# FFN weight scales from ScalarE's sums of squares, x's transposes issued one tile later, the product copies in a buffer of their own, and the queues laid out anew

## The chip, the cores and the metric

The kernel runs on one core of a Trainium2 chip. A core has TensorE (in the profile PE for its matmuls, PEld for its weight loads), VectorE (DVE), ScalarE (ACT), GpSimd (POOL) and SyncE (SP, whose work is to issue DMAs). Each engine takes its instructions in the order in which the program lists them. The metric is the device time of one execution, in microseconds. Lower is better.

## The reference

The input x has 2048 rows of 576. It is normalised, goes through windowed attention with 32 heads of 18, and the result is gated by a bilinear feed-forward network (FFN) of width 4608.

```python
# _A_ref: qkv = x @ wqkv; softmax over the last 256 positions, causal; ... @ wo
# _B_ref:
    g = jnp.einsum("bsd,df->bsf", x, w_gate)
    u = jnp.einsum("bsd,df->bsf", x, w_up)
    h = g * u
    return jnp.einsum("bsf,fd->bsd", h, w_down)
# the whole:
    x = A_x
    xn = _layernorm(x, axis=-1)
    s = _A_ref(xn, A_wqkv, A_wo)
    g = _silu(_B_ref(xn, B_w_gate, B_w_up, B_w_down))
    return x + s * g
```

All inputs and outputs are float32.

## The kernel before

**Arithmetic.** Every float32 matrix is split into two float16 matrices, a high part and a low part, and a product is made of three float16 matmuls (high by high, high by low, low by high). So that the parts fit float16, each weight matrix is first multiplied by a power of two. `power` works it out from a bound on the matrix's largest magnitude: it clears the mantissa bits and takes the reciprocal. The high part is made by ScalarE (`hi`, L139), the low part by VectorE (`lo`, L142), which subtracts the high part from the scaled source.

**Prologue.** The rows of x come in 16 tiles of 128. For a tile, `stats`, `root` and `newton` give mean and deviation, `norm2` writes the normalised tile and its split `xh` (ScalarE, and GpSimd for the low part, L222 and L223), and `turn` (L226) transposes `xh` into `XT` by a DMA that SyncE issues. V is made tile by tile (`v_pass`, L307). Then q and k are made for the first 1024 rows (half 0) and later for the other 1024 (half 1): `qk_tile` runs 14 matmuls for one of 9 blocks of 128 columns (m) and one of two blocks of 512 rows, ScalarE and VectorE write the result into the tile `qp` (two buffers), and `qk_store` (L353) sends the finished tile m to DRAM in eight DMAs. Between two of these blocks `aside` does other work. In half 0 it is the preparation of x's tiles 8 to 15 through `pair`, whose step number n grows by one from block to block: `stats` at 0 and 1, `norm2` and `turn` of the first tile at 2, of the second at 3. In half 1 it is, among others, the first FFN group's scale (`ffn_amax`, `ffn_spread_out`, `ffn_spread_in`, `ffn_scale`). `keep_warm` runs matmuls on zeros whose result nobody reads. At the very start TensorE takes `v_full(0)` and `v_full(1)` (L500), then `spread_pe` (L447), which brings the bound of V's weights to one partition.

**Memory.** The prologue's tiles lie in the pools `qpool` and `pro`, which are closed behind the last q/k block. The pool `late` and the attention pool are opened in the same memory, so a tile of theirs waits until the tiles that lay there have had their last use. `late` holds the FFN's accumulator `acc`, the split down weights `dnw`, the hidden values `hh` and the ring `ft` of four tiles of 128x512, into which the FFN's products are copied. `const` and `ring` are open throughout.

**Main loop.** There are 72 slots: 18 groups of 256 FFN columns (g), and in each group four slots (two blocks of 128 columns, k, by two halves of 1024 rows, q). A slot computes seven products P1 to P7 into the two PSUM banks A and C (`prod`, `mm`, L844). The products come out of the banks by ScalarE's `copy_out` (L872) and VectorE's `add_out` (L876) and `times_0` (L880); GpSimd's `times_1` (L884) makes the second half of the hidden values; `h_hi` (L888) and `h_lo` (L892) split them. Eight `down` units (L908) of three slots before run in between, each drained by `down_out` (L918, L920) on VectorE; most share one bank `dn`. Slots 1 to 64 also carry one attention step each: scores (L715), maxima (`score`, L724), exponentials (`probs`, L729 and L731), their split (`probs_hi` L736, `turn_probs` L745 with a transposing DMA L748), the product with V (`weigh`, L757) and `finish` (L769 to L778).

The weights of group g are loaded three slots ahead of its first slot (`ffn_raw`), that is in a slot whose number is 1 modulo 4. Their bounds are taken there and in the slot behind it (`ffn_amax`, L372: six reductions to the largest magnitude, three matrices by two halves; `ffn_spread_out`, L377, combines the halves and stores them; `ffn_spread_in` reads them back on all partitions; `ffn_scale`, L385 and `power`, makes the scales). GpSimd then forms scaled sums of the weights (`ffn_ratio` L393, `ffn_sums` L404). The splits of the weights (`w_hi`, `w_lo`, `dn_hi`, `dn_lo`, `dn_low`) stand in the slots 3 and 0 modulo 4, and one of them in 1.

**Order.** The order on every engine is set by hand: `at(slot, t, f, ...)` gives each call a due time of slot x 18.65 + t, and the list is sorted by it. The times of most calls that are not matmuls stand in the table `W`. They set the order alone; an instruction runs when its engine reaches it and its inputs are there.

```python
    for n in range(6):
        at(b - 3, W["amax"][n], ffn_amax, g, (1, 1, 2, 2, 0, 0)[n], n % 2)
    at(b - 3, W["so"], ffn_spread_out, g)
    at(b - 3, W["si"], ffn_spread_in, g)
    at(b - 2, W["scale"], ffn_scale, g)
```

Of the kernel before, what the change touches and what calls it, by code (L numbers as in the profile page):

```python
# [8 lines left out]
F32 = mybir.dt.float32  # L9
FR = mybir.dt.float32r  # L10
BF = mybir.dt.bfloat16
F16 = mybir.dt.float16
AF = mybir.ActivationFunctionType
OP = mybir.AluOpType
AX = mybir.AxisListType
# [5 lines left out]
def kernel(  # L21
# [10 lines left out]
    nc = tc.nc  # L32
    x = x[0]
    out = out[0]
    S, D = x.shape
# [9 lines left out]
    scale = DH ** -0.5  # L45
# [11 lines left out]
    WF = 2.0 ** 12  # L57
# [5 lines left out]
    LEAST, MOST = 2.0 ** -60, 2.0 ** 60  # L63
# [22 lines left out]
    ps_o = const.tile([128, 4], F32, name="ps_o")  # L86
    sig = const.tile([128, 4], F32, name="sig")

    def wq_ring():
        return pro.tile([128, 10, 128], F16, name="wq", bufs=9)  # L90

# [11 lines left out]
    def keep_warm(n):  # L103
        ps = bank("pv", 1)
        for _ in range(n):
            nc.tensor.matmul(ps, idle[:, 0:128], idle, start=True, stop=True)
# [5 lines left out]
    def power(m, p, s, top):  # L112

        nc.vector.tensor_scalar(p, m, LEAST, MOST, op0=OP.max, op1=OP.min)
        pi = p.bitcast(mybir.dt.int32)
        nc.vector.tensor_scalar(pi, pi, 0x7F800000, None, op0=OP.bitwise_and)
        nc.vector.reciprocal(s, p)
        nc.vector.tensor_scalar(s, s, top, None, op0=OP.mult)

# [105 lines left out]
    def turn(t):  # L225
        nc.sync.dma_start(XT[:, :, t * 128:(t + 1) * 128], XH.pop(t), transpose=True)  # L226
# [97 lines left out]
    UW, DW, RAW, SC, SW = {}, {}, {}, {}, {}  # L324
# [42 lines left out]
    def ffn_amax(g, kind, half):  # L367
        if (g, "am") not in SC:
            SC[g, "am"] = ring.tile([128, 2, 3], F32, name="am", bufs=2)
        r = RAW[g, kind]  # L370
        r = r[:, half] if kind == 2 else r[:, :, half * 128:(half + 1) * 128]
        nc.vector.tensor_reduce(SC[g, "am"][:, half, kind:kind + 1], r, axis=AX.X if kind == 2 else AX.XY,  # L372
                                op=OP.max, apply_absolute_value=True)

    def ffn_spread_out(g):
        am = SC.pop((g, "am"))
        nc.vector.tensor_tensor(am[:, 0], am[:, 0], am[:, 1], op=OP.max)  # L377
        spread_out(f"f{g}", am[:, 0], 3)

    def ffn_spread_in(g):  # L380
# [2 lines left out]
    def ffn_scale(g):  # L383
        sc = SC[g] = ring.tile([128, 12], F32, name="sc", bufs=3)
        nc.vector.tensor_reduce(sc[:, 0:3], SC.pop((g, "sp")), axis=AX.X, op=OP.max)  # L385
        power(sc[:, 0:3], sc[:, 3:6], sc[:, 6:9], WF)
        nc.gpsimd.tensor_tensor(sc[:, 10:11], sc[:, 3:4], sc[:, 7:8], op=OP.mult)
        nc.gpsimd.tensor_tensor(sc[:, 9:10], sc[:, 3:4], sc[:, 4:5], op=OP.mult)
        nc.gpsimd.tensor_scalar(sc[:, 9:10], sc[:, 9:10], sc[:, 5:6], C_FFN, op0=OP.mult, op1=OP.mult)
# [55 lines left out]
    def spread_pe(col, k):  # L445
        tp = bank("dn", 1)
        nc.tensor.transpose(tp[0:1, 0:128], col, ident)  # L447
        nc.vector.tensor_reduce(mrow[:, k:k + 1], tp[0:1, 0:128], axis=AX.X, op=OP.max)
# [46 lines left out]
    def v_full(k):  # L495
        if k == 0:
            PV[0] = [bank(*VB[j]) for j in range(2)]
        r = slice(0, 128 if k < 4 else 64)
        for j in range(2):
            nc.tensor.matmul(PV[0][j][:, :HALF], x32[r, k], rv[r, k, j * HALF:(j + 1) * HALF],  # L500
                             start=k == 0, stop=k == 4)

    for k in range(2):
        v_full(k)
    spread_pe(ps_v[:, 0:1], 0)
    norm2(2)
    turn(2)
# [56 lines left out]
    def pair(p, n):  # L564

        if n == 1:
            stats(2 * p + 1)
            root(2 * p, 2)
            newton(2 * p, 2)
        elif n == 0:  # L570
            stats(2 * p)
        elif n in (2, 3):
            norm2(2 * p + n - 2)
            turn(2 * p + n - 2)

    def aside(half, n):

# [22 lines left out]
    for t in range(16):  # L600
        if t % 8 > 3 or t >= 8:
            v_pass(t, 0, 4)
            if t == 7:
                tp = spread_pe2(1, "up", 2)
            v_pass(t, 4, 14)
            if t == 6:
                spread_pe(am_qk[:, 5:6], 1)
            if t == 6:
                v_store(0)
            if t == 7:  # L610
                qk_scale(tp)
                x_load(8)
                x_load(9)
        if t % 8 > 0 and t > 2:
            v_out(t - 1)
        if t in (2, 4):
            amax(am_qk[:, t // 2:t // 2 + 1], rqk[:, t // 2])
        elif t in (3, 5):
            k = (t + 5) // 2 - 1
            square(am_qk[:, k:k + 1], rqk[:, k])  # L620
        if t == 5:
            nc.scalar.activation(am_qk[:, 3:5], am_qk[:, 3:5], AF.Sqrt)
            nc.vector.tensor_reduce(am_qk[:, 5:6], am_qk[:, 0:5], axis=AX.X, op=OP.max)
        if t >= 8:
            for p in range(4):
                t_form(p, t - 8 - 2 * p)
        if t % 8 < 7:
            continue
        half = t // 8
        if half == 0:  # L630
            qk_split(0)
            qk_split(1)
        v_out(t)
        for m in range(QM):
            for c in (2 * half, 2 * half + 1):
                qk_tile(UW["q", m], m, c)
                aside(half, 2 * m + c % 2)
            qk_store(m, half)
            if half == 0:
                if m < 7:  # L640
                    v_store(m + 1)
                if m in (0, 2, 4):
                    x_load(10 + m)
                    x_load(11 + m)
                if m == 8:
                    for kind in range(3):
                        for part in range(2):
                            ffn_raw(0, kind, part)
            else:
                if m == 2:  # L650
                    ffn_spread_out(0)
                if m == 3:
                    ffn_spread_in(0)
                del UW["q", m]
# [8 lines left out]

    def h_ring():
        return late.tile([128, 2, 512], F16, name="hh", bufs=8)

    def f_ring():
        return late.tile([128, 512], F32, name="ft", bufs=4)

    att = att_stack.enter_context(tc.tile_pool(name="att", bufs=1))  # L670
    bias = att.tile([128, 384], BF, name="bias")
# [119 lines left out]

    NSLOT = NG * NCH
    T = 18.65
    W = {"ttr": [-1.02, -0.99, 2.9, 3.58, 7.44, 8.28, 9.7, 10.61], "exp": [0.73, 4.02, 9.94, 10.85], "cast": [1.61, 4.85, 10.71, 12.76], "plo": [3.33, 6.32, 12.48, 13.35], "fin": 8.64, "whi": [6.17, 10.44, 7.03, 16.67], "wlo": [9.12, 13.19, 15.36, 18.08], "dhi": 16.48, "dlo": 18.02, "dlow": 18.26, "sum0": [15.56, 19.68, 19.83], "sum1": [-8.02, 0.5, 6.85], "amax": [11.14, 11.93, 14.37, 14.25, 18.11, 18.75], "scale": 14.47, "hhi0": 18.41, "hlo0": 22.9, "hhi1": 21.52, "hlo1": 23.66, "h1": 18.28, "pv": [16.98, 7.67], "x": 7.18, "raw0": 11.17, "so": 21.83, "si": 24.97}
    todo = []

    def at(slot, t, f, *a):
# [325 lines left out]
```

## Time and profile before

| | us |
|---|---|
| median of 3 runs | 1631.88 |
| lowest, highest | 1630.68, 1631.97 |
| the profiled execution, whole | 1631.18 |
| its span in the profile | 1629.5 |

The profile is that of one execution. The page gives busy time by engine; the timeline gives instructions in order of time, merged where they are alike, with the idle time of the engine ahead of them and what ended it in brackets (`[2.76 <-DVE qp L344]`); the groups give for each line and shape the count, the busy time, the mean duration in ns, and behind a bar the idle time before; the view of one line gives the least, median and greatest duration in ns. `L844` is line 844 of the kernel. The ends of matmuls are modelled and overlap a little.

### The profile page before, as it was taken

To read this page: it belongs to the slowest core of one execution; us is meant where nothing else is said; L and a number is where in the kernel's file an instruction comes from. 1 tells how busy PE (TensorE), PEld (TensorE's weight loads), DVE (VectorE), ACT (ScalarE), POOL (GpSimd) and SP (SyncE) were. 2 spreads that over 40 slices of the span, in tenths; PEclk is the share of its full clock that TensorE was granted. 3 is DMA by queue.
4 is the path that set the end of the run, shared out by engine and by line. 5 is a ranking of instruction groups with operands and counts; after the bars stand their busy time and mean duration, and the time that the engine had idled before them with its cause. 6 is when DMAs were issued, how large, how long until landed. Compare 5 with 4: busy or idle time off the path is not lost.

```text
span 1629.5 us, 32463 instructions
## 1 busy us (share of the span) xinstructions
PE 1585.4 (97%) x11875; PEld 905.3 (56%) x11875; DVE 1360.3 (83%) x2989; ACT 923.2 (57%) x1742; POOL 815.0 (50%) x823
## 2 busy tenths in 40 slices
PE   9999989999999999999999999999999999999999
PEld 5455335555555555555555555555555555555577
DVE  7546478898989899998989898999998999977564
ACT  6433366565666666576666566666666666623230
POOL 3122346555565757565656566665656574723000
PEclk9999999999999999999999999999999999999999
DMA  8473365555647576857666666666675757540435
GB/s 235 116 181 126 88 125 109 110 118 110 130 82 152 114 159 107 169 105 150 127 131 138 124 133 133 135 132 141 126 145 109 160 108 157 106 115 2 103 79 170
DMA packets 551457, 206.06 MB, mean 126 GB/s; under 512 B 492544, under 2 KB 532096, under 8 KB 551296
## 3 DMA queue, kind: packets, MB, share of 16 engines
q1 hardware_dynamic: 551296, 203.98, 59.0%
q8 instruction: 93, 1.52, 0.4%
q14 instruction: 68, 0.56, 0.1%
HBM read 76.63 MB, written 23.75 MB: 62 GB/s over the span
## 4 chain that ended last, share of the span: by engine, by line
PE 47%; DVE 29%; issue 4%; DMA 3%; ACT 2%; SPq 1%; POOL 0%; ACTq 0%; DVEq 0%; POOLq 0%
PE up L844 25%; PE dn L908 9%; PE s L908 6%; DVE acc L920 5%; DVE ws L142 4%; DVE ft L876 3%; PE pv L757 3%; DVE hh L892 3%; DVE wu L142 2%; PE s L1013 2%; DVE dnw L142 2%; PE s L715 2%; DMA raw<-in_B_w_gate_dram 2%; PE up L1013 1%; DVE am L372 1%
## 5 line engine op out<-in xcount | busy, mean ns | idle before, releaser
L908 PEld LDWEIGHTS <-hh 128*128 128x128 f16 x3456 | 329.1, 98 | 180.6 <-issue 25.5
L908 PE MATMUL dn<-dnw,hh 128*128 128x288 f16 x2070 | 310.3, 286 | 14.7 <-DVE acc L920 14.0
L844 PEld LDWEIGHTS <-ws 128*128 128x128 f16 x1872 | 178.2, 98 | 187.5 <-issue 32.1
L844 PE MATMUL up<-XT,ws 128*128 128x512 f16 x1008 | 273.2, 381 | 1.2 <-DVE ft L876 1.2
L844 PE MATMUL up<-XT,wg 128*128 128x512 f16 x1008 | 254.6, 382 | 1.5 <-DVE ft L880 1.2
L844 PE MATMUL up<-TX,ws 128*128 128x512 f16 x864 | 211.6, 381 | 6.1 <-ACT ft L872 6.1
L888 ACT ACTIVATE hh<-ft 128x512 f16<-128x512 f32 x144 | 90.6, 629 | 221.6 <-DVE ft L880 219.8
L920 DVE SCALAR_TENSOR_TENSOR acc<-dn,sc,acc 128x288 f32<-128x288 f32 x325 | 166.1, 511 | 53.6 <-PE dn L908 53.0
L908 PE MATMUL s<-dnw,hh 128*128 128x288 f16 x1386 | 203.9, 286 | 0.0
L876 DVE SCALAR_TENSOR_TENSOR ft<-up,ft 128x512 f32<-128x512 f32 x216 | 147.4, 683 | 32.4 <-PE up L844 26.9
L872 ACT ACTIVATE ft<-up 128x512 f32<-128x512 f32 x216 | 126.4, 585 | 83.5 <-PE up L844 75.7
L729 ACT ACTIVATE mx<-mx 128x2 f32<-128x2 f32 x256 | 52.0, 203 | 195.7 <-DVE mx L724 194.5
L884 POOL TENSOR_TENSOR ft<-ft 128x512 f32<-128x512 f32 x72 | 92.5, 1285 | 135.1 <-DVE ft L876 102.8
L892 DVE SCALAR_TENSOR_TENSOR hh<-hh,ft 128x512 f16<-128x512 f16 x144 | 149.9, 1041 | 0.2 <-ACT hh L888 0.2
L844 PEld LDWEIGHTS <-wg 128*128 128x128 f16 x1008 | 99.2, 98 | 84.8 <-issue 5.7
L920 DVE SCALAR_TENSOR_TENSOR acc<-s,sc,acc 128x288 f32<-128x288 f32 x219 | 111.6, 510 | 27.2 <-PE s L908 27.1
L844 PEld LDWEIGHTS <-wu 128*128 128x128 f16 x720 | 70.1, 97 | 94.1 <-issue 30.5
L339 PE MATMUL up<-XT,wq 128*128 128x512 f16 x504 | 111.4, 383 | 6.0 <-DVE qp L344 5.9
L757 PEld LDWEIGHTS <-pt 128*128 128x128 f16 x2880 | 86.2, 96 | 47.6 <-issue 30.2
L844 PE MATMUL up<-TX,wu 128*128 128x512 f16 x432 | 105.0, 379 | 0.0
L844 PE MATMUL up<-XT,wu 128*128 128x512 f16 (+1 forms) x288 | 98.0, 381 | 0.0
L757 PE MATMUL pv<-vt,pt 128*128 128x37 f16 x2880 | 93.4, 179 | 0.8 <-DMA vt<-v_d 0.8
(1225 smaller groups left out, 2774.6 us busy)
## 6 DMA issues: line engine op xcount, KB each, us to landing
raw<-in_B_w_down_dram SPq DMA_DIRECT2D x36, 288.0 KB
raw<-in_B_w_gate_dram SPq DMA_DIRECT2D x36, 256.0 KB
raw<-in_B_w_up_dram SPq DMA_DIRECT2D x36, 256.0 KB
qk_d<-qp SPq DMA_DIRECT2D x112, 72.0 KB
vt<-v_d SPq DMA_DIRECT2D x48, 111.0 KB
ks<-qk_d SPq DMA_DIRECT2D x96, 54.0 KB
v_d<-vo SPq DMA_DIRECT2D x16, 296.0 KB
xr<-in_A_x_dram SPq DMA_DIRECT2D x16, 288.0 KB
```

Of the source, the lines that this page charges most:

```text
L142: nc.vector.scalar_tensor_tensor(w, rv, s, h, op0=OP.mult, op1=OP.subtract)
L339: nc.tensor.matmul(ps, a, b, start=i == 0, stop=i == len(pl) - 1)
L729: nc.scalar.activation(mx[:, 2:4], mx[:, 0:2], AF.Copy, bias=shift)
L757: nc.tensor.matmul(PVB[s][:, j, i, :VW], pt[:, 2 * nb * j + n], VT[s][:, lo_ + n % nb, j * VW:(j + 1) * VW], start=n == 0, stop=n == 2 * n ...
L844: nc.tensor.matmul(ps.rearrange("p (m n) -> p m n", n=128), w, b, start=start, stop=stop, skip_group_check=True)
L872: nc.scalar.activation(FT[sl, name], BK[bk], AF.Copy, scale=E_SC)
L876: nc.vector.scalar_tensor_tensor(f, BK[bk], E_SC, f, op0=OP.mult, op1=OP.add)
L884: nc.gpsimd.tensor_tensor(f, f, FT[sl, "a3"], op=OP.mult)
L888: nc.scalar.activation(hh[:, 0], FT[sl, ("a1", "a2")[c]], AF.Copy, scale=1.0 / LO)
L892: nc.vector.scalar_tensor_tensor(hh[:, 1], hh[:, 0], -LO, FT[sl, ("a1", "a2")[c]], op0=OP.mult, op1=OP.add)
L908: nc.tensor.matmul(ps[:, :HALF], a, b, start=n == 0, stop=n == len(l) - 1)
L920: nc.vector.scalar_tensor_tensor(d, ps[:, :HALF], SC[g][:, 9:10], d, op0=OP.mult, op1=OP.add)
```

## The change

1. `ffn_amax` takes no largest magnitude on VectorE any more. ScalarE squares the same six blocks and accumulates the sum over each row; the squares themselves go to a throw-away tile that shares its buffer with `spread`. `ffn_spread_out` adds the two halves on GpSimd instead of taking their maximum on VectorE. The bound is thus a sum of squares, and `root_power` takes the place of `power` in `ffn_scale`: it halves the exponent by shifts and has one VectorE instruction more.
2. In `pair` the calls of `turn` move from steps 2 and 3 to steps 4 and 5, so each is issued two blocks later, behind the store of a q/k tile that it stood ahead of. The last of them falls behind half 0 and is issued after V's first pass of the second half.
3. The ring `ft` moves from the pool `late` to `const`.
4. Six matmuls on zeros stand ahead of `spread_pe`.
5. All times of the table `W` are new.

```diff
--- before.py
+++ after.py
@@ -86,6 +86,9 @@
     ps_o = const.tile([128, 4], F32, name="ps_o")
     sig = const.tile([128, 4], F32, name="sig")
 
+    def f_ring():
+        return const.tile([128, 512], F32, name="ft", bufs=4)
+
     def wq_ring():
         return pro.tile([128, 10, 128], F16, name="wq", bufs=9)
 
@@ -114,6 +117,15 @@
         nc.vector.tensor_scalar(p, m, LEAST, MOST, op0=OP.max, op1=OP.min)
         pi = p.bitcast(mybir.dt.int32)
         nc.vector.tensor_scalar(pi, pi, 0x7F800000, None, op0=OP.bitwise_and)
+        nc.vector.reciprocal(s, p)
+        nc.vector.tensor_scalar(s, s, top, None, op0=OP.mult)
+
+    def root_power(m, p, s, top):
+
+        nc.vector.tensor_scalar(p, m, LEAST * LEAST, MOST * MOST, op0=OP.max, op1=OP.min)
+        pi = p.bitcast(mybir.dt.int32)
+        nc.vector.tensor_scalar(pi, pi, 24, 23, op0=OP.logical_shift_right, op1=OP.logical_shift_left)
+        nc.vector.tensor_scalar(p, p, 2.0 ** 64, None, op0=OP.mult)
         nc.vector.reciprocal(s, p)
         nc.vector.tensor_scalar(s, s, top, None, op0=OP.mult)
 
@@ -367,14 +379,18 @@
     def ffn_amax(g, kind, half):
         if (g, "am") not in SC:
             SC[g, "am"] = ring.tile([128, 2, 3], F32, name="am", bufs=2)
-        r = RAW[g, kind]
-        r = r[:, half] if kind == 2 else r[:, :, half * 128:(half + 1) * 128]
-        nc.vector.tensor_reduce(SC[g, "am"][:, half, kind:kind + 1], r, axis=AX.X if kind == 2 else AX.XY,
-                                op=OP.max, apply_absolute_value=True)
+            junk_ = ring.tile([128, 128, 3], F32, name="spread", bufs=1).rearrange("p a n -> p (a n)").bitcast(BF)
+            SC[g, "junk"] = junk_
+        r, j = RAW[g, kind], SC[g, "junk"]
+        if kind == 2:
+            r, j = r[:, half], j[:, 0:D]
+        else:
+            r, j = r[:, :, half * 128:(half + 1) * 128], j[:, 0:640].rearrange("p (k n) -> p k n", n=128)
+        nc.scalar.activation(j, r, AF.Square, accum_out=SC[g, "am"][:, half, kind:kind + 1])
 
     def ffn_spread_out(g):
         am = SC.pop((g, "am"))
-        nc.vector.tensor_tensor(am[:, 0], am[:, 0], am[:, 1], op=OP.max)
+        nc.gpsimd.tensor_tensor(am[:, 0], am[:, 0], am[:, 1], op=OP.add)
         spread_out(f"f{g}", am[:, 0], 3)
 
     def ffn_spread_in(g):
@@ -383,7 +399,7 @@
     def ffn_scale(g):
         sc = SC[g] = ring.tile([128, 12], F32, name="sc", bufs=3)
         nc.vector.tensor_reduce(sc[:, 0:3], SC.pop((g, "sp")), axis=AX.X, op=OP.max)
-        power(sc[:, 0:3], sc[:, 3:6], sc[:, 6:9], WF)
+        root_power(sc[:, 0:3], sc[:, 3:6], sc[:, 6:9], WF)
         nc.gpsimd.tensor_tensor(sc[:, 10:11], sc[:, 3:4], sc[:, 7:8], op=OP.mult)
         nc.gpsimd.tensor_tensor(sc[:, 9:10], sc[:, 3:4], sc[:, 4:5], op=OP.mult)
         nc.gpsimd.tensor_scalar(sc[:, 9:10], sc[:, 9:10], sc[:, 5:6], C_FFN, op0=OP.mult, op1=OP.mult)
@@ -502,6 +518,7 @@
 
     for k in range(2):
         v_full(k)
+    keep_warm(6)
     spread_pe(ps_v[:, 0:1], 0)
     norm2(2)
     turn(2)
@@ -571,7 +588,8 @@
             stats(2 * p)
         elif n in (2, 3):
             norm2(2 * p + n - 2)
-            turn(2 * p + n - 2)
+        elif n in (4, 5):
+            turn(2 * p + n - 4)
 
     def aside(half, n):
 
@@ -621,6 +639,8 @@
         if t == 5:
             nc.scalar.activation(am_qk[:, 3:5], am_qk[:, 3:5], AF.Sqrt)
             nc.vector.tensor_reduce(am_qk[:, 5:6], am_qk[:, 0:5], axis=AX.X, op=OP.max)
+        if t == 8:
+            pair(7, 5)
         if t >= 8:
             for p in range(4):
                 t_form(p, t - 8 - 2 * p)
@@ -664,9 +684,6 @@
     def h_ring():
         return late.tile([128, 2, 512], F16, name="hh", bufs=8)
 
-    def f_ring():
-        return late.tile([128, 512], F32, name="ft", bufs=4)
-
     att = att_stack.enter_context(tc.tile_pool(name="att", bufs=1))
     bias = att.tile([128, 384], BF, name="bias")
     nc.gpsimd.memset(bias, 0.0)
@@ -791,7 +808,7 @@
 
     NSLOT = NG * NCH
     T = 18.65
-    W = {"ttr": [-1.02, -0.99, 2.9, 3.58, 7.44, 8.28, 9.7, 10.61], "exp": [0.73, 4.02, 9.94, 10.85], "cast": [1.61, 4.85, 10.71, 12.76], "plo": [3.33, 6.32, 12.48, 13.35], "fin": 8.64, "whi": [6.17, 10.44, 7.03, 16.67], "wlo": [9.12, 13.19, 15.36, 18.08], "dhi": 16.48, "dlo": 18.02, "dlow": 18.26, "sum0": [15.56, 19.68, 19.83], "sum1": [-8.02, 0.5, 6.85], "amax": [11.14, 11.93, 14.37, 14.25, 18.11, 18.75], "scale": 14.47, "hhi0": 18.41, "hlo0": 22.9, "hhi1": 21.52, "hlo1": 23.66, "h1": 18.28, "pv": [16.98, 7.67], "x": 7.18, "raw0": 11.17, "so": 21.83, "si": 24.97}
+    W = {"ttr": [-1.15, -1.05, 2.52, 2.83, 7.3, 7.88, 8.43, 10.52], "exp": [-0.32, 3.27, 10.53, 11.29], "cast": [2.01, 4.58, 10.96, 13.04], "plo": [3.91, 6.4, 12.99, 14.37], "fin": 8.7, "whi": [7.57, 12.02, 10.92, 16.48], "wlo": [8.87, 15.17, 11.54, 18.48], "dhi": 15.41, "dlo": 18.04, "dlow": 18.47, "sum0": [17.15, 22.33, 23.83], "sum1": [-12.14, 0.91, 8.29], "amax": [11.76, 10.5, 18.31, 16.62, 20.43, 19.12], "scale": 13.08, "hhi0": 18.26, "hlo0": 23.0, "hhi1": 21.96, "hlo1": 25.11, "h1": 19.18, "pv": [18.2, 8.25], "x": 7.03, "raw0": 10.0, "so": 21.25, "si": 23.98}
     todo = []
 
     def at(slot, t, f, *a):
```

## The prediction

> **What bounds the kernel now.** I read the page first.
>
> ```profile
> span 1629.5 us, 32463 instructions
> ...
> PE 1585.4 (97%) x11875; PEld 905.3 (56%) x11875; DVE 1360.3 (83%) x2989; ACT 923.2 (57%) x1742; POOL 815.0 (50%) x823
> ```
>
> TensorE is busy 97% of the span, so only its waits and its stretched work can be won. They lie in three places, which the timeline and the busy time by stretches show. The first is the early projection: the 252 matmuls of q and k for the first half of the rows, with the same 252 of the second half in the last row.
>
> ```profile
> 46.05 24.34 PE L339 MATMUL up<-XT,wq 128*128 128x512 f16 x112
> 73.15 13.93 PE L339 MATMUL up<-XT,wq 128*128 128x512 f16 x56 [2.76 <-DVE qp L344]
> 88.10 12.52 PE L339 MATMUL up<-XT,wq 128*128 128x512 f16 x56 [1.02 <-DVE qp L344]
> 102.75 6.20 PE L339 MATMUL up<-XT,wq 128*128 128x512 f16 x28 [2.14 <-DVE qp L344]
> 136.23 54.55 PE L339 MATMUL up<-XT,wq 128*128 128x512 f16 x252
> ```
>
> 46.05 to 108.95 is 62.9 us, against 54.55 us without a wait: 8.35 us lost, of which 5.92 are waits; most of the rest is the slow stretch after the first wait (56 matmuls in 13.93 us, later 12.52).
>
> The second is slot 0 of the main loop, up to 209.11, with slot 1 behind it:
>
> ```profile
> 190.62 3.46 PE L844 MATMUL up<-XT,wg 128*128 128x512 f16 x14
> 198.03 2.72 PE L844 MATMUL up<-TX,ws 128*128 128x512 f16 x6 [3.94 <-ACT ft L872]
> 204.83 1.46 PE L844 MATMUL up<-TX,wu 128*128 128x512 f16 x6
> 209.11 3.18 PE L844 MATMUL up<-XT,wg 128*128 128x512 f16 x14 [0.61 <-DVE ft L880]
> 223.49 3.18 PE L844 MATMUL up<-XT,wg 128*128 128x512 f16 x14 [0.21 <-DVE ft L880]
> ```
>
> The third is the loop. Below are four slots in a row, of kind 3, 0, 1, 2 (their number modulo 4). Then stands the stretch of slots 16 to 63, which all have full attention tiles.
>
> ```profile
> 847.50:867.24 19.74, 19.27 (x156) 10.83 (x154) 18.50 (x40) 14.25 (x26) 14.42 (x15) 1.00 0.52 100
> 867.24:887.11 19.87, 19.21 (x156) 10.84 (x154) 19.78 (x39) 13.44 (x25) 13.35 (x14) 1.00 0.60 101
> 887.11:905.86 18.75, 18.75 (x157) 10.75 (x154) 17.70 (x42) 11.77 (x22) 9.08 (x8) 1.00 0.82 191
> 905.86:927.38 21.52, 19.54 (x157) 10.90 (x155) 18.20 (x45) 11.09 (x21) 10.44 (x12) 0.98 0.79 134
> ```
> ```profile
> 481.20:1411.20 930.00, 914.88 (x7383) 517.94 (x7382) 864.18 (x1900) 605.51 (x1129) 566.05 (x541) 1.00 0.67 133
> ```
>
> The columns are length, then busy time of PE, PEld, DVE, ACT and POOL. The slot of kind 1 takes 18.75 us with TensorE busy all through: that is TensorE's own pace. 48 slots at it are 900 us and the stretch takes 930, so 30 us are lost, 2.5 per group of four. In the kind 0 slot DVE is busy 19.78 of 19.87 us: it bounds the slot.
>
> **The change part by part.** *Turns two steps later* (`pair`). SyncE issues in order; before, a turn stood ahead of the store of the finished tile m.
>
> ```profile
> 59.75 0.68 DVE L344 SCALAR_TENSOR_TENSOR qp<-up,qp 128x512 f16<-128x512 f32 x1
> 63.05 2.51 SPq L226 DMA_TRANSPOSE XT<-xh  x1
> 65.66 3.13 SPq L353 DMA_DIRECT2D qk_d<-qp  x8
> 71.78 0.60 ACT L343 ACTIVATE qp<-up 128x512 f16<-128x512 f32 x1 [6.08 <-DMA qk_d<-qp]
> ```
>
> Tile m=1 is complete at 60.4, but its eight stores go out only from 65.66 to 68.79, behind the turn. Their buffer is free at 71.78, 3.0 us after the last issue. In the new order the stores go at about 60.5 to 63.6 and the buffer is free at 66.6; at an undisturbed pace (54.55/18 = 3.03 us per tile) the first copy of m=3 comes at 46.05 + 7 x 3.03 = 67.3. No wait is left, with 0.7 us to spare. The turn then stands ahead of the next store; the same sum for m=4 (turn to 66.1, stores to 69.2, free at 72.2, needed at 73.3) also closes. The last turn now also stands behind the first FFN weight loads and the first V pass; what needs it is the last of the eight V passes. Gain 8.3 us; between 0 (the wait only changes its transfer) and 8.35. I take 8.3, since every step closes.
>
> *keep_warm(6).*
>
> ```profile
> 9.38 2.21 PE L500 MATMUL s<-rv,wq 128*128 128x288 f32 x8 [0.20 <-ACT wq L477]
> 13.61 0.27 PE L447 MATMUL dn<-ident,ps_v 128*1 128x128 f32 x1 [2.02 <-DVE ps_v L493]
> 15.09 4.28 PE L500 MATMUL s<-rv,wq 128*128 128x288 f32 x8
> 19.30 3.77 PE L307 MATMUL up<-wv,XT 128*128 128x288 f16 x18
> 22.91 2.37 PE L307 MATMUL s<-wv,XT 128*128 128x288 f16 x18
> 23.11 2.27 DVE L142 SCALAR_TENSOR_TENSOR wv<-rv,ps_v,wv 128x576 f16<-128x576 f32 x3
> ```
>
> After the 2.02 us wait eight matmuls take 4.28 us that took 2.21 before it, and eighteen take 3.77 against 2.37. Six matmuls at the loop's 0.22 us (54.55/252) are 1.3 us and fit into the 2.02 us. If they hold the pace, TensorE is 3.5 us earlier (4.28 - 2.21 and 3.77 - 2.37), but V's low weights are only done at 25.4 (23.11 + 2.27). Twenty more matmuls of 0.13 us (2.37/18) follow the last row's eighteen, to about 27.7; the last four need the last low weight and cannot end before about 25.9. So at most about 1.7 is won. If they run at half pace (2.6 us) they delay the spread by 0.6. So -1.7 to +0.6; I take -1.
>
> *ft in its own buffer.* Slot 0's second product waits for the first copy out:
>
> ```profile
> 197.38 0.60 ACT L872 ACTIVATE ft<-up 128x512 f32<-128x512 f32 x1 [4.93 <-DMA ks<-qk_d]
> ```
>
> The copy writes memory that the prologue's pool still held, whose last users are the q/k stores. In `const` nothing holds it: ScalarE is free at 192.45 (197.38 - 4.93). The 3.94 us wait goes, and with it the slow matmuls (2.72 against 1.46 us for six). Late next are the copies that slot 1 shows: it takes 14.38 us (209.11 to 223.49), slot 0 18.49. If slot 0 becomes like slot 1, 4.1 us are won; at most 3.94 plus about 2.5 of slow pace, 6.4. I take 5.
>
> *Sums of squares on ScalarE.*
>
> ```profile
> L372 DVE TENSOR_REDUCE am<-raw x108: 737/810/820, 142.9 to 1449.7; 128x1 f32<-128x640 f32 x72, 128x1 f32<-128x576 f32 x36
> L377 DVE TENSOR_TENSOR am<-am x18: 153/1572/1576, 158.1 to 1450.8; 128x3 f32<-128x3 f32 x18
> L257 ACT ACTIVATE wq<-rv x2: 667/680/694, 10.0 to 12.4; 128x576 bf16<-128x576 f32 x2
> L257 ACT ACTIVATION_READ_ACCUMULATOR wq<-rv x2: 187/194/200, 10.6 to 12.9; 128x1 f32 x2
> ```
>
> DVE loses 4 x 0.81 + 2 x 0.74 + 1.57 = 6.3 us per group, in slots of kind 1 and 2; `root_power` adds one tiny DVE instruction (0.15 alone, up to 1.57 by the L377 row). ScalarE gains six of 0.68 (0.76 for 640) + 0.19, 5.5 us per group: 3.7 in kind 1 (11.77 to 15.5 of 18.75), 1.8 in kind 2 (11.09 to 12.9). ScalarE has room. The last two squares wait for the gate weights, and behind them stand copy a1 and, for its bank, P6; the load is due at 10.0 of the slot before and these squares 9.1 and 10.4 later, where the reductions came 6.9 and 7.6 behind a load due at 11.17, so I count no wait. The add goes to POOL at 0.15 to 1.57 us; it waits for the last square, and behind it stand POOL's first attention subtract and that tile's transpose on SyncE, which the idle half of POOL (10.44 of 21.52) covers.
>
> *The queues.* Kinds 3 and 0, where the splits stand, lose nothing of their work. What can shrink there is DVE held by POOL:
>
> ```profile
> 871.82 1.56 DVE L892 SCALAR_TENSOR_TENSOR hh<-hh,ft 128x512 f16<-128x512 f16 x1
> 871.18 1.65 POOL L745 TENSOR_TENSOR pp<-sm__11753,pp 128x768 f16<-128x768 f32 x1
> 876.47 0.90 PE L908 MATMUL dn<-dnw,hh 128*128 128x288 f16 x6 [0.55 <-DVE acc L920]
> L892 DVE SCALAR_TENSOR_TENSOR hh<-hh,ft 128x512 f16<-128x512 f16 x96 | 111.8, 1164 | 0.0
> 886.58 0.60 DVE L724 CUSTOM_DVE_ANT_0 sm__12038<-s,bias,sig 128x384 f32<-128x384 f32 x1
> 922.44 0.67 DVE L385 TENSOR_REDUCE sc<-spread 128x3 f32<-128x384 f32 x1 [1.12 <-DMA spread<-sd_f]
> ```
>
> A 128x512 subtract takes 0.68 with one PSUM operand (59.75) but 1.16 on average as L892, where it begins beside a POOL subtract: some 0.48 x 96 = 46 us. TensorE then waits for a drained bank (876.47). The Trainium skill, "SBUF — State Buffer", Who interferes with whom, says that a VectorE instruction with two SBUF inputs contends with a GpSimd instruction reading SBUF, one blocking the other, while on trn2 a reduce never contends. The trace agrees: the reduces stay within 737 to 820. By that rule taking reduces away shortens no hold, and with nothing from the layout the sum would be 1631.2 - 14.3 - 0.4 x 12 = 1612.
>
> In the new layout the first sums' split is due at 11.54, ahead of the POOL subtract at 12.99, and the split of up at 15.17, behind the one at 14.37; they were at 15.36 and 13.19, with POOL at 12.48 and 13.35. The two hh subtracts stay close to POOL's first two. So some holds go, not all. The spread back is due ahead of the k loads, at 5.33 instead of 6.32, which ends the 1.12 us wait and the 21.52 us slot. One or two score reductions (0.60 each) now precede add a2, which was due at 17.6; the bank it frees is wanted 2.03 into the next slot, 3.1 later, so this hides unless DVE is more than about a microsecond behind.
>
> Loop: of 2.5 us per group, 1.0 and 1.1 are in kinds 3 and 0 (19.74 and 19.87 less 18.75), about 0.4 on average in kind 2. I take kind 2 whole and half of the others: 0.4 + 1.05 = 1.45, times 12 = 17. Bounds: +29 (below) and -30.
>
> **Sum** against the profiled run's own 1631.2 us (span 1629.5 and 1.7 around it; 0.7 under the median of 1631.9): 8.3 + 1 + 5 + 17 = 31.3, so 1600.
>
> **The rivals.** *The loop does not move*: holds fall as they did, DVE's freed time lies in slots with idle time already (kind 1: 17.70 of 18.75). 1631.2 - 14.3 = 1617. For it: kinds 3 and 0 keep their work. Against: kind 2's wait is on the removed chain.
>
> *All waits go*: 8.3 + 1.7 + 6.4 + 30 = 46.4, so 1585. Against it: the hh subtracts.
>
> *The turn's wait is handed on* to later stores: 1600 + 8.3 = 1608.
>
> *Slower: more holds.* With DVE full in kind 0, one hold more of about 1.2 us (at most POOL's 1.65) in each split slot goes straight to TensorE: 24 x 1.2 = 29, so 1631.2 - 14.3 + 29 = 1646. It decides from 14.3/24 = 0.6 us more per split slot. Against: two splits moved away from POOL's subtracts.
>
> *Table switches.*
>
> ```profile
> 210.45 1.28 ACT L731 ACT_TABLE_LOAD   x1
> ```
>
> If Square needed another table than Exp, the squares' four stretches between exponentials would cost 8 x 1.28 = 10.2 us per group, 7.7 in kind 1: 15.5 + 7.7 is 4.4 over 18.75, times 17 groups 75, so about 1675. Square ran under the Sqrt table with no load of its own, which speaks against it. The Trainium skill, "ScalarE: Activation LUTs", Table sets: the hidden batching unit, says cheap functions stand in every set but does not list Square; no run here shows it under Exp.
>
> **How the numbers follow.** Forecast 1600: 0.52; no loop gain 1617: 0.19; all waits 1585: 0.16; handed on 1608: 0.05; more holds 1646: 0.06; tables 1675: 0.02. The range 1583 to 1620 leaves out the last two and the edges. About 0.2%, 3.3 us, can be told from no change. Faster 0.91, same 0.02, slower 0.07.
>
> **What would show it.** Right: one unbroken block of 252 matmuls early; slot 0 near 14 us; kind 2 slots at 18.8; L892's mean under 1.16. Wrong: [.. <-DVE qp] waits still there, kind 0 slots still at 19.87 or longer with DVE full, table loads in the loop, or TensorE waiting for ft by ScalarE behind a square.

## The result and the profile after

The changed kernel (called after from here on) takes 1607.51 us (median of 4 runs, 1606.69 to 1608.40), the kernel before 1631.93 beside it: a ratio of 0.9852, 95% interval 0.9835 to 0.9869. That is faster by 24.4 us, with 31.3 forecast. The profiled execution spans 1605.3 us, where that of before spans 1629.5.

The page's line of busy times, then the windows of four slots of kind 3, 0, 1, 2 and of slots 16 to 63. Their columns are length, busy time of PE, PEld, DVE, ACT and POOL, then the granted clock, the DMA share and GB/s:

```profile
PE 1567.0 (98%) x11881; PEld 901.2 (56%) x11881; DVE 1224.2 (76%) x2881; ACT 982.6 (61%) x1958; POOL 843.0 (53%) x841
```
```profile
832.40:851.20 18.80, 18.80 (x163) 10.82 (x160) 15.85 (x38) 14.03 (x26) 15.36 (x14) 1.00 0.68 104
851.20:870.80 19.60, 18.85 (x159) 10.69 (x155) 17.13 (x39) 13.35 (x25) 13.59 (x13) 1.00 0.58 103
870.80:890.50 19.70, 18.95 (x163) 10.80 (x160) 16.02 (x38) 13.80 (x29) 10.01 (x7) 1.00 0.86 197
890.50:909.20 18.70, 18.70 (x159) 10.72 (x156) 14.49 (x41) 12.57 (x27) 10.61 (x12) 1.00 0.73 131
```
```profile
467.20:1387.90 920.70, 903.35 (x7389) 516.17 (x7386) 760.75 (x1825) 644.49 (x1273) 590.67 (x552) 1.00 0.68 134
```

Kinds 3 and 2 now run at TensorE's own pace. Kinds 0 and 1 do not: TensorE is idle for 0.75 us in each, and DVE is far from full (17.13 of 19.60). Kind 1, which had lost next to nothing before, now loses as much as kind 0.

The prologue and the first slots of the main loop, TensorE's timeline:

```profile
45.60 48.51 PE L351 MATMUL up<-XT,wq 128*128 128x512 f16 x224
94.69 6.20 PE L351 MATMUL up<-XT,wq 128*128 128x512 f16 x28 [0.58 <-DVE qp L356]
...
182.56 3.46 PE L861 MATMUL up<-XT,wg 128*128 128x512 f16 x14
...
194.47 3.18 PE L861 MATMUL up<-XT,wg 128*128 128x512 f16 x14 [0.61 <-DVE ft L897]
...
209.82 3.18 PE L861 MATMUL up<-XT,wg 128*128 128x512 f16 x14 [0.21 <-DVE ft L897]
214.76 1.46 PE L861 MATMUL up<-TX,ws 128*128 128x512 f16 x6 [1.75 <-ACT ft L889]
```

Read from the starts of such rows in both traces, the 24.2 us between the two spans come from these places: up to the q/k block 0.45; the block itself 7.6 (62.74 to 55.13, by the start of the matmul behind it); slot 0 6.6 (18.49 to 11.91); slots 1 to 3 1.05; slots 4 to 15 a loss of 1.7; slots 16 to 63 9.3; what follows 0.8.

Where kinds 0 and 1 wait, by the timelines of DVE, POOL and PE at the start of a slot of kind 0:

```profile
850.21 0.61 DVE L741 CUSTOM_DVE_ANT_0 sm__11754<-s,bias,sig 128x384 f32<-128x384 f32 x1
...
850.74 0.61 DVE L741 CUSTOM_DVE_ANT_0 sm__11754<-s,bias,sig 128x384 f32<-128x384 f32 x1
...
851.28 0.69 DVE L893 SCALAR_TENSOR_TENSOR ft<-up,ft 128x512 f32<-128x512 f32 x1
851.88 0.81 DVE L154 SCALAR_TENSOR_TENSOR dnw<-raw,sc,dnw 128x576 f16<-128x576 f32 x1
852.61 1.90 DVE L154 SCALAR_TENSOR_TENSOR ws<-sums,sc,ws 128x640 f16<-128x640 f32 x1
854.43 0.50 DVE L937 SCALAR_TENSOR_TENSOR acc<-dn,sc,acc 128x288 f32<-128x288 f32 x1
```
```profile
852.05 1.77 POOL L901 TENSOR_TENSOR ft<-ft 128x512 f32<-128x512 f32 x1 [1.83 <-DVE ft L893]
```
```profile
854.99 0.90 PE L925 MATMUL dn<-dnw,hh 128*128 128x288 f16 x6 [0.75 <-DVE acc L937]
```

Two score reductions (L741) stand ahead of add a2 (L893), the `add_out` that completes a factor of the second half's product. Add a2 releases POOL's product `times_1` (L901), which now runs beside the split of the second sums (L154, ws). The split takes 1.90 us; behind it in DVE's queue stands the drain of the down bank (L937), and for that bank TensorE waits. The next slot, of kind 1, shows the same, with 1.77, 1.89 and 0.75.

Before, at the same place, add a2 came first of the same five instructions, and the product was over before the split began, DVE and POOL:

```profile
866.11 0.68 DVE L876 SCALAR_TENSOR_TENSOR ft<-up,ft 128x512 f32<-128x512 f32 x1
...
868.67 0.87 DVE L142 SCALAR_TENSOR_TENSOR ws<-sums,sc,ws 128x640 f16<-128x640 f32 x1
869.47 0.51 DVE L920 SCALAR_TENSOR_TENSOR acc<-dn,sc,acc 128x288 f32<-128x288 f32 x1
```
```profile
866.86 1.27 POOL L884 TENSOR_TENSOR ft<-ft 128x512 f32<-128x512 f32 x1 [1.18 <-DVE ft L876]
```

### The profile page after: what moved, and what is told of

It is laid out like the page before. It is cut to its first block, busy times and chain, and to the rows that moved or that the text cites. A ratio compares the mean times of both kernels' runs of the same rounds, so it can differ in the third digit from the quotient of the medians.

```text
span 1605.3 us, 32691 instructions
## 1 busy us (share of the span) xinstructions
PE 1567.0 (98%) x11881; PEld 901.2 (56%) x11881; DVE 1224.2 (76%) x2881; ACT 982.6 (61%) x1958; POOL 843.0 (53%) x841
## 4 chain that ended last, share of the span: by engine, by line
PE 75%; DVE 10%; issue 1%; DMA 1%; POOL 0%; SPq 0%; ACT 0%; DVEq 0%; POOLq 0%
PE up L861 42%; PE dn L925 15%; PE s L925 9%; PE pv L774 3%; DVE ws L154 3%; PE s L732 2%; DVE dnw L154 2%; PE s L1030 2%; PE up L1030 1%; DVE ft L893 1%; DVE acc L937 1%; DVE ft L897 0%; DMA spread<-sd_f 0%; DMA sd_f<-am 0%; DMA vt<-v_d 0%
## 5 line engine op out<-in xcount | busy, mean ns | idle before, releaser
L937 DVE SCALAR_TENSOR_TENSOR acc<-dn,sc,acc 128x288 f32<-128x288 f32 x325 | 166.2, 511 | 76.8 <-PE dn L925 76.2
L901 POOL TENSOR_TENSOR ft<-ft 128x512 f32<-128x512 f32 x72 | 106.0, 1473 | 163.0 <-DVE ft L893 131.8
L893 DVE SCALAR_TENSOR_TENSOR ft<-up,ft 128x512 f32<-128x512 f32 x216 | 148.0, 685 | 42.2 <-PE up L861 38.8
L937 DVE SCALAR_TENSOR_TENSOR acc<-s,sc,acc 128x288 f32<-128x288 f32 x219 | 112.5, 514 | 74.9 <-PE s L925 74.7
L861 PEld LDWEIGHTS <-wg 128*128 128x128 f16 x1008 | 93.6, 97 | 79.5 <-issue 1.8
L909 DVE SCALAR_TENSOR_TENSOR hh<-hh,ft 128x512 f16<-128x512 f16 x144 | 123.3, 857 | 15.5 <-ACT hh L905 15.2
L774 PEld LDWEIGHTS <-pt 128*128 128x128 f16 x2880 | 91.1, 96 | 18.9 <-DMA vt<-v_d 0.6
```

The costliest lines, as they stand in the source:

```text
L774: nc.tensor.matmul(PVB[s][:, j, i, :VW], pt[:, 2 * nb * j + n], VT[s][:, lo_ + n % nb, j * VW:(j + 1) * VW], start=n == 0, stop=n == 2 * n ...
L861: nc.tensor.matmul(ps.rearrange("p (m n) -> p m n", n=128), w, b, start=start, stop=stop, skip_group_check=True)
L893: nc.vector.scalar_tensor_tensor(f, BK[bk], E_SC, f, op0=OP.mult, op1=OP.add)
L901: nc.gpsimd.tensor_tensor(f, f, FT[sl, "a3"], op=OP.mult)
L909: nc.vector.scalar_tensor_tensor(hh[:, 1], hh[:, 0], -LO, FT[sl, ("a1", "a2")[c]], op0=OP.mult, op1=OP.add)
L937: nc.vector.scalar_tensor_tensor(d, ps[:, :HALF], SC[g][:, 9:10], d, op0=OP.mult, op1=OP.add)
```

## The experiments

The kernel before took 1628.80 to 1629.64 us beside the experiments and 1631.93 beside the changed kernel, so differences between an experiment and the changed kernel are good to about 3 us. Where less matters, stretches of the traces are compared: slots 16 to 63 take 920.62 us in the changed kernel and, to the hundredth, in the run with the turns back. The diffs are cut at "...".

**The reductions behind add a2.** After, with the first two score reductions due later:

```diff
-    W = {"ttr": [-1.15, -1.05, 2.52, ...
+    W = {"ttr": [-1.02, -0.99, 2.52, ...
```

> The changed kernel with one thing undone: the first two score reductions of a step stand again behind the second half's last drain (add a2), at -1.02 and -0.99 as before. Theory: in the changed kernel add a2 comes about 1.1 us later, so GpSimd's product (times_1) starts while VectorE makes the low part of the weight sums, VectorE is held about 1.1 us, and the drain of down unit 7 behind it comes too late for down unit 1. Then the 0.75 us waits in the slots of kind 0 and 1 go, some 0.9 us in each of two slots of 17 groups: about 28 us, so some 1580 us. Rival: the split itself, held or not, stands ahead of the drain and makes it late; then the waits stay and the time stays within 3 us of 1607.5.

Measured: 1585.38 us (1584.5 to 1587.5), ratio to before 0.9735 [0.9720, 0.9749]: 22 us faster than the changed kernel, by two numbers of its table. The same place, DVE and POOL:

```profile
839.05 0.68 DVE L893 SCALAR_TENSOR_TENSOR ft<-up,ft 128x512 f32<-128x512 f32 x1
...
840.72 0.99 DVE L154 SCALAR_TENSOR_TENSOR dnw<-raw,sc,dnw 128x576 f16<-128x576 f32 x1
841.63 0.87 DVE L154 SCALAR_TENSOR_TENSOR ws<-sums,sc,ws 128x640 f16<-128x640 f32 x1
842.43 0.51 DVE L937 SCALAR_TENSOR_TENSOR acc<-dn,sc,acc 128x288 f32<-128x288 f32 x1
```
```profile
839.82 1.27 POOL L901 TENSOR_TENSOR ft<-ft 128x512 f32<-128x512 f32 x1 [0.75 <-DVE ft L893]
```

The product now runs beside the reductions and is over (841.09) before the split of the second sums begins: 0.87 instead of 1.90. Slots 16 to 63 take 901.8 us; 48 at TensorE's pace of 18.75 are 900.

**The same order put into the kernel before.**

```diff
-    W = {"ttr": [-1.02, -0.99, 2.9, ...
+    W = {"ttr": [-1.15, -1.08, 2.9, ...
```

> The kernel before with one part of the new times alone: the first two score reductions due at -1.15 and -1.08, so ahead of add a2. Theory: GpSimd's product starts about 1.1 us later and holds the split on VectorE; down unit 1 waits about 0.75 us in the slots of kind 0 and 1 of 15 groups and more: 15 to 28 us slower, some 1650. Rival, that this order is harmless without the other new times: within 3 us of 1632.

Measured: 1644.82 us (1640.93 to 1646.55), ratio 1.0092 [1.0068, 1.0116], 16 us slower. The split and the wait are as long as in after, to the hundredth, DVE and PE:

```profile
870.75 1.90 DVE L142 SCALAR_TENSOR_TENSOR ws<-sums,sc,ws 128x640 f16<-128x640 f32 x1
```
```profile
873.13 0.90 PE L908 MATMUL dn<-dnw,hh 128*128 128x288 f16 x6 [0.75 <-DVE acc L920]
```

POOL's product takes 1.77 again (870.19 to 871.96). So the order alone makes the wait, with or without the rest of the change.

**Order or meeting?** In every order so far both reductions stand ahead of the drain; what the two experiments above move is add a2, and with it the start of the product. This one keeps the reductions ahead of add a2, so the product starts as late as in after, and moves the split ahead of them, so that it is done before the product starts. DVE has the same five instructions before the drain:

```diff
-    ... "wlo": [8.87, 15.17, 11.54, 18.48], ...
+    ... "wlo": [8.87, 15.17, 11.54, 17.45], ...
```

> After, with the second sums' split due at 17.45 (was 18.48), so it stands ahead of the two score reductions, which keep their early place ahead of add a2. VectorE does the same work ahead of down_out7 as in after; only the meeting of the split with GpSimd's product times_1 is gone. Theory (the held split, 1.90 us beside the product against some 0.8 without it, is what makes TensorE wait): the 0.75 us waits in slots of kind 0 and 1 go, 28 x 0.75 = 21 us, about 1586. Rival (the two reductions, 2 x 0.6 us ahead of add a2, are enough): the waits stay, 1607. In between: GpSimd's sums, released earlier by the split, meet other subtracts, 1590 to 1600.

Measured: 1583.45 us (1583.45 to 1585.07), ratio 0.9714 [0.9693, 0.9735], the fastest kernel here. DVE and POOL:

```profile
837.35 0.88 DVE L154 SCALAR_TENSOR_TENSOR ws<-sums,sc,ws 128x640 f16<-128x640 f32 x1
838.14 0.61 DVE L741 CUSTOM_DVE_ANT_0 sm__11755<-s,bias,sig 128x384 f32<-128x384 f32 x1
...
839.22 0.69 DVE L893 SCALAR_TENSOR_TENSOR ft<-up,ft 128x512 f32<-128x512 f32 x1
839.82 0.81 DVE L154 SCALAR_TENSOR_TENSOR dnw<-raw,sc,dnw 128x576 f16<-128x576 f32 x1
840.55 0.52 DVE L937 SCALAR_TENSOR_TENSOR acc<-dn,sc,acc 128x288 f32<-128x288 f32 x1
```
```profile
839.99 1.78 POOL L901 TENSOR_TENSOR ft<-ft 128x512 f32<-128x512 f32 x1 [2.62 <-DVE ft L893]
```

The reductions ahead of add a2 cost nothing here. From the start of the first of the five instructions to the drain it is 4.22 us in after (850.21 to 854.43), 3.36 before, 3.38 with the reductions moved (839.05 to 842.43) and 3.20 here (837.35 to 840.55). The meeting of the second sums' split and the product is what cost the time. The product still meets the other split ahead of the drain (dnw, which ends at 840.63) and takes 1.78, but that split came first and is not held (0.81).

**The split behind the drain.** After, with the split due later instead:

```diff
-    ... "wlo": [8.87, 15.17, 11.54, 18.48], ...
+    ... "wlo": [8.87, 15.17, 11.54, 18.8], ...
```

> The changed kernel with the last low part of the weight sums due at 18.8 instead of 18.48, so behind the drain of down unit 7 (18.65) and no longer ahead of it. Theory: the wait of down unit 1 for that drain goes, whatever holds the split: 0.9 us in each of two slots of 17 groups, about 28 us, so some 1580 us; the split is still held by GpSimd's product (about 1.9 us). Rival: the time held only moves on, to the drain of unit 0 and the next reductions, and the slots of kind 0 and 1 stay at 19.66 us: 1607.

Measured: 1600.0 us (1598.67 to 1602.46), ratio 0.9824 [0.9810, 0.9839], between the two expectations. Kind 1 is clean at 18.74, but kind 0 rises to 20.28 on average. DVE and PE in a slot of kind 0 that starts at 996.95:

```profile
998.80 1.47 DVE L154 SCALAR_TENSOR_TENSOR ws<-sums,sc,ws 128x640 f16<-128x640 f32 x1
...
1002.12 1.91 DVE L909 SCALAR_TENSOR_TENSOR hh<-hh,ft 128x512 f16<-128x512 f16 x1
...
1004.56 2.12 DVE L909 SCALAR_TENSOR_TENSOR hh<-hh,ft 128x512 f16<-128x512 f16 x1
```
```profile
1007.16 0.90 PE L925 MATMUL dn<-dnw,hh 128*128 128x288 f16 x6 [0.85 <-DVE acc L937]
```

The split is still held (1.47), POOL's next sums wait for it until 1000.35, and the POOL work behind them runs beside both hh subtracts, which take 1.91 and 2.12 us. TensorE waits for the drain behind them.

**Both orders together**: the reductions behind add a2 and the split at 18.8.

> After, with the two reductions behind add a2 (due -1.02 and -0.99) and also the second sums' split behind down_out7 (due at 18.8). If the late split alone shifts GpSimd's sums into the hh subtracts of kind 0 (1.91 and 2.12 us there against 1.49 and less), the waits of kind 0 come back: slots of kind 0 at 20.3, about 1585 + 12 x 1.5 = 1603. If with add a2 earlier everything keeps clear: kinds 0 and 1 at 18.74 and slots 4 to 15 without their 0.36 us waits, about 1581.

Measured: 1595.24 us (1593.68 to 1597.27), ratio 0.9784 [0.9764, 0.9804]. Slots 4 to 15 take 219.4 us against 222.2 with the reductions alone moved, as the second expectation has it; kind 0 rises to 19.87, in the direction of the first. The two cures of the same wait together are worse than the moved reductions alone (1585.38) or the early split (1583.45).

**Maxima back on VectorE.** `ffn_amax`, `ffn_spread_out` and the call of `root_power` as before; everything else of after kept:

```diff
-        nc.scalar.activation(j, r, AF.Square, accum_out=SC[g, "am"][:, half, kind:kind + 1])
+        nc.vector.tensor_reduce(SC[g, "am"][:, half, kind:kind + 1], r, axis=AX.X if kind == 2 else AX.XY,
+                                op=OP.max, apply_absolute_value=True)
```

> The changed kernel with the weight bounds again as largest magnitudes, reduced on VectorE at the new due times (and the old scale from them); all else as changed. Theory: the reductions fall into slots of kind 1 and 2, where VectorE is idle 3.7 and 4.2 us in the changed kernel, and 6.3 us per group do not quite fit: at most 2 us per group, 1607 to 1635; I expect 1612. Rival, that the whole gain of the loop comes from taking them off VectorE: the loop's 9.3 us come back or more, 1617 and above.

Measured: 1609.70 us (1609.21 to 1611.66), ratio 0.9885 [0.9869, 0.9902]; its slots 16 to 63 take 922.6 us, after's 920.6. Under the new table the squares bring about 2 us, by the loop; the medians differ by as much, which is less than they can tell.

**The old table.** After with all due times of before:

```diff
-    W = {"ttr": [-1.15, -1.05, 2.52, 2.83, ...
+    W = {"ttr": [-1.02, -0.99, 2.9, 3.58, ...
```

> The changed kernel with the table of due times of before; squares on ScalarE, turns, zeros and the ft ring as changed. Theory: the holds of the splits and of the hh subtracts by GpSimd come back in the slots of kind 3 and 0 (19.7 and 19.9 us), kind 1 is at 18.75 again and kind 2 near 18.75: the loop stretch of slots 16 to 63 about 922 us, as in the changed kernel by chance, and the whole near 1608. Rival, that the new times carry the loop's gain: the stretch goes back to 930 and the whole to 1617.

Measured: 1624.39 us (1620.49 to 1627.83), ratio 0.9968 [0.9957, 0.9980], above both expectations. Slots 16 to 63 take 937.8 us in the profiled execution, 8 more than before took; this execution was the longest of nine, 3.4 us over their median. DVE, POOL and PE at the end of a slot of kind 2:

```profile
1071.50 1.56 DVE L127 TENSOR_SCALAR sc<-sc 128x3 int32<-128x3 int32 x1
...
1073.59 0.51 DVE L937 SCALAR_TENSOR_TENSOR acc<-s,sc,acc 128x288 f32<-128x288 f32 x1
```
```profile
1071.40 1.64 POOL L762 TENSOR_TENSOR pp<-sm__14832,pp 128x768 f16<-128x768 f32 x1 [2.06 <-ACT pp L753]
```

```profile
1074.15 0.32 PE L732 MATMUL s<-ks,qs 54*128 54x384 f16 x1 [1.16 <-DVE acc L937]
```

The shift on three numbers in `root_power` ends when POOL's attention subtract ends, the drain waits behind it, and TensorE waits for the drain.

**The squares alone.** Whether that loss is the squares' own: before, with the new `ffn_amax`, `ffn_spread_out` and `root_power`, and nothing else.

> Before, with the sums of squares on ScalarE, the add on GpSimd and root_power, and nothing else; the due times are the old ones. It leaves VectorE 6.3 us per group of four less to do. Theory (from the kernel after under the old times, whose loop of slots 16 to 63 took 937.8 us against 929.9 before, and whose slot 2 lost some 4 us to a copy behind a square that waits for the gate weights): slower, about 1637. Rival (that loss came with the other parts): within 3 us of before or faster, 1625 to 1632.

Measured: 1636.3 us (1632.08 to 1637.72), ratio 1.0037 [1.0021, 1.0052], 6.7 us slower although DVE has 6.3 us less to do per group. The groups of DVE in slots 16 to 63, and ScalarE and TensorE in slot 2:

```profile
L905 DVE SCALAR_TENSOR_TENSOR hh<-hh,ft 128x512 f16<-128x512 f16 x96 | 130.5, 1360 | 0.6 <-ACT hh L901 0.5
```
```profile
226.56 0.74 ACT L386 ACTIVATE spread<-raw 128x640 bf16<-128x640 f32 x1 [2.10 <-DMA raw<-in_B_w_gate_dram]
```
```profile
229.98 2.63 PE L857 MATMUL up<-TX,ws 128*128 128x512 f16 x6 [3.76 <-ACT ft L885]
```

The hh subtracts are held longer than before: a mean of 1360 ns against 1164, 18.7 us in sum. In slot 2 the copies (the first at 229.35) stand behind squares that wait for the gate weights.

**The turns back.** After with `turn` at steps 2 and 3 again:

```diff
-        elif n in (4, 5):
-            turn(2 * p + n - 4)
+            turn(2 * p + n - 2)
...
-        if t == 8:
-            pair(7, 5)
```

> The changed kernel with the turns of x's tiles 8 to 15 back at steps 2 and 3 of the preparation, ahead of the store of the finished q/k tile. Theory: the three waits of TensorE for q/k copies come back (5.9 us and a slow stretch after the first); the first half's q/k block goes from 55.1 to about 62.7 us and the whole from 1607.5 to about 1615. Rival, that the earlier start of the stores came from something else (the zeros, other DMA traffic): no change.

Measured: 1614.39 us (1613.21 to 1615.28), ratio 0.9901 [0.9882, 0.9921], 6.9 us more than after. Waits of 1.15, 0.61, 2.23 and 1.97 us are back in TensorE's timeline; the longest:

```profile
87.27 12.25 PE L351 MATMUL up<-XT,wq 128*128 128x512 f16 x56 [2.23 <-DVE qp L356]
```

**The ring ft back in `late`.**

```diff
-        return const.tile([128, 512], F32, name="ft", bufs=4)
+        return late.tile([128, 512], F32, name="ft", bufs=4)
```

> The changed kernel with the ft ring back in the pool that opens behind the prologue. Theory: slot 0's first copy waits again until the last q/k stores have left that memory; slot 0 goes from 11.9 to about 18.5 us and the whole from 1607.5 to about 1613.5. Rival, that slot 0 got shorter by the new times or by the earlier stores: it stays under 13 us, no change.

Measured: 1614.35 us (1612.29 to 1615.25), ratio 0.9900 [0.9880, 0.9919], 6.8 more than after; slot 0 takes 18.73 us again. ScalarE and TensorE:

```profile
189.81 0.60 ACT L889 ACTIVATE ft<-up 128x512 f32<-128x512 f32 x1 [4.95 <-DMA ks<-qk_d]
```
```profile
190.46 2.72 PE L861 MATMUL up<-TX,ws 128*128 128x512 f16 x6 [3.96 <-ACT ft L889]
```

**Without the zeros.** After without `keep_warm(6)`.

> The changed kernel without the six matmuls on zeros. Theory: the granted clock falls to half behind the 2 us wait again, about 3.4 us of slow matmuls come back, but XT's transposes and V's low weights bound the start of V anyway, so the q/k block starts only about 0.5 us later: 1608. Rival, that the full 3.4 us are on the path: 1611.

Measured: 1607.22 us (1606.11 to 1610.0), ratio 0.9860 [0.9840, 0.9881]: no difference that can be told. Its profiled execution shows the slower stretch that the zeros avoid; granted clock 0.50 against 1.00 in the same window of after, first without, then with the zeros:

```profile
15.10:25.20 10.10, 10.10 (x32) 5.82 (x31) 8.64 (x22) 5.85 (x12) 5.08 (x7) 0.50 0.88 243
```
```profile
15.10:25.20 10.10, 9.33 (x62) 6.28 (x62) 9.76 (x24) 6.64 (x12) 5.23 (x8) 1.00 1.09 267
```

That execution took 1610.0 us, the longest of its four, and its slot 0 begins at 184.75, where that of after begins at 182.56; the medians show none of these 2.2 us.

## Why the prediction was right, and where it was not

The direction and the range held: 1607.5 in 1583 to 1620. It is also the time of the rival "handed on" (1608), but not for its reason: of the turn's waits only 0.58 us is left. The loop's term carries the error, and that it is no larger is luck: a gain that was counted too small met a loss that was not counted.

*Loop, 17 forecast, 9.3 measured.* The step that failed is "One or two score reductions (0.60 each) now precede add a2 [...] so this hides unless DVE is more than about a microsecond behind". It followed add a2 to the bank that it frees, and not to the product on POOL that it releases. The early split shows that the reductions alone do hide. The product, 1.2 us later, meets the split, which takes 1.90 us where it takes 0.87, and the drain comes 0.84 later (4.22 against 3.38). TensorE waits up to 1.06 us for it in each slot of kinds 0 and 1, 24 waits and 17.4 us of the 20.6 that slots 16 to 63 still lose; over the whole kernel the reductions moved back are worth 22.

By the starts of the slots in both traces, the 12 slots of kind 3 won 8.8 us, those of kind 2 8.2 and those of kind 0 2.9, and those of kind 1, which the sum leaves out, lost 10.6. The sum had read 1.0, 1.1 and 0.4 us as the losses of kinds 3, 0 and 2 from one group; over the 12 groups they were 0.72, 1.07 and 0.68.

The other half of that step held. "Two splits moved away from POOL's subtracts" was right: the split of the first sums goes from 1869 to 740 ns on average, and the split of up from 1551 to 609, as its groups before and after show. The hh subtracts, of which "some holds go, not all", go from 1164 to 890 ns.

```profile
L142 DVE SCALAR_TENSOR_TENSOR wu<-raw,sc,wu 128x384 f16<-128x384 f32 x24 | 37.2, 1551 | 0.0
```
```profile
L154 DVE SCALAR_TENSOR_TENSOR wu<-raw,sc,wu 128x384 f16<-128x384 f32 x24 | 14.6, 609 | 0.0
```

Without the new meeting the term would have been 28, beyond the half of kinds 3 and 0 that was counted: the rival "all waits go" (1585) is what the two cured kernels reach, 1585.38 and 1583.45. The rival "more holds" (1646, chance 0.06) comes nearest to the mechanism, a POOL instruction that holds one split more in two slots of four; it was thought of for slots in which DVE is full. The order that makes it, put alone into the kernel before, costs 16 us.

*What would show it.* Kind 2 is at 18.70, where the text said 18.8 of a right forecast. Kind 0 stayed near 19.87, at 19.60, as it said of a wrong one, but not "with DVE full": DVE has 2.5 us to spare. An engine with idle time can still deliver late.

*Turns, 8.3 forecast, 7.6 in the trace and 6.9 undone.* The order on SyncE is as worked out, with stores at 60.02 where they stood at 65.66; one wait of 0.58 us stayed, at the last tile. There the sum did not close: the stores that free the buffer went out from 86.52 to 89.94, behind a turn issued at 84.25, and the copy into it began at 93.32.

*ft, 5 forecast, 6.6 in the trace and 6.8 undone.* Slot 0 became shorter than slot 1 (11.9 against 15.4), the upper bound of the sum (6.4) and a little more; slot 1 has twice the ScalarE work (13.3 us against 6.5), and the estimate took the one for the other.

*keep_warm, 1 forecast.* 0.45 in the trace, nothing in the times. With the clock kept, V's next passes wait for x's transposes instead, by 0.46 us and by 1.38:

```profile
34.15 3.60 PE L319 MATMUL up<-wv,XT 128*128 128x288 f16 x28 [1.38 <-DMA XT<-xh]
```

*Squares, 0 forecast.* Nearly so: they bring 2 us under the new table, by the loop. "I count no wait" was wrong once: in slot 2 a copy (at 214.13) stands behind a square that waits for the gate weights, which is TensorE's 1.75 us wait above:

```profile
213.39 0.74 ACT L389 ACTIVATE spread<-raw 128x640 bf16<-128x640 f32 x1 [1.48 <-DMA raw<-in_B_w_gate_dram]
```

That DVE's removed work gains nothing was right, and the squares alone even lose.

## What to carry to other kernels

When an instruction moves in one queue, follow what its end releases on every other engine, and ask which instruction that work will now run beside; here the delayed add was harmless and the product it released was not. An engine that loses work is not thereby earlier where it counts, and its other instructions can then be held for longer, as the hh subtracts were with the squares alone. Two numbers of a hand-made table were worth 22 us, almost as much as the whole change: after a new layout, undo its steps one at a time at the place where a queue still waits.

## What the runs showed of the hardware

*A split on DVE and a product on POOL wait for each other, in turn.* By the code each of them reads two inputs from SBUF. In after the product begins at 852.05, while DVE's dnw split runs to 852.69, and takes 1.77 us where it takes 1.27 beside the reductions. Counted from the split's end it needs 1.1, to 853.82. The ws split begins at 852.61 and ends at 854.51; counted from the product's end it needs 0.7, near the 0.87 that it takes undisturbed. In the early-split run it is 1.14 from the end of the dnw split (840.63) to that of the product (841.77). So, as far as these ends tell, each waited for the other to finish, and their delays chain. The Trainium skill, "SBUF — State Buffer", Who interferes with whom, says that the port they share is an exclusive lock and that issue order decides who blocks. The trace agrees, with 1.77 against 1.27 and 1.90 against 0.87; the reductions, whose scores come from PSUM, stay at 0.61 beside the product.

*A three-element instruction is held too.* Under the old table the shift of `root_power` took 1.56 us beside POOL's attention subtract, and ended with it (1073.06 and 1073.04), although it has one input; in after it takes 0.17 each time:

```profile
L127 DVE TENSOR_SCALAR sc<-sc x18: 168/170/170, 161.5 to 1437.1; 128x3 int32<-128x3 int32 x18
```

The same section of the Trainium skill names `tensor_scalar` among the operations that can take the shared port for a mode of their own; the trace agrees that it can be held, with these 1.56 us.

*Square under Exp's table.* The squares run between exponentials throughout the loop without a table load of their own: the trace of after has three loads, at 0.78, at 195.20 ahead of the first exponential, and at 1529.90, while the exponentials end at 1401.79 and the squares at 1426.92. The rival of 1675 us is gone.

```profile
195.20 1.28 ACT L748 ACT_TABLE_LOAD   x1
```

What stays open: why the early split leaves a wait of up to 0.44 us in three slots of kinds 0 and 1, and why the old table's loop loses more in kinds 2 and 3 with the squares than the held shift explains.
